# Gated mix of segment attention and a gated MLP: the order of the first loads, of four key transposes and of some dummy matmuls is changed

## The chip, the cores and the metric

One core of a Trainium2 chip runs the whole kernel. The metric is device time in microseconds (us) of one execution; before the change the median of three runs is 287.96 us (287.41 to 287.99).

## The reference, cut to what matters

The input `x` has 2048 tokens of 512 features in bf16. Two branches read it and are mixed by one gate per token.

```
g = sigmoid(sum(x * gate_w))                       # one number per token
out = g * A(x) + (1 - g) * B(x)
A: q, k, v = x@wq, x@wk, x@wv; 32 heads of 16; 4 segments of 512 tokens
   for each segment s:
     a_dot = softmax(q k^T / 4 + causal mask) v    # inside the segment
     a_mem = phi(q) M / (phi(q) z + 1e-6)          # memory of the earlier segments
     o = sigmoid(beta) * a_mem + (1 - sigmoid(beta)) * a_dot
     M += phi(k)^T v;  z += sum(phi(k))            # phi(t) = t+1 if t>0 else exp(t)
   A = o @ wo
B: h = relu(x@W_gate) * (x@W_up)   (1792 wide);  B = h @ W_down
```

## The kernel before

Everything stays in SBUF. `xT` holds x transposed (features on partitions) in four chunks of 512 tokens, one per segment. The work of segment s is: the projections `proj(s)` (L550), attention `att(s)` (L643: 20 "quads" of scores, an exponential of 128x2048 on ScalarE for each, a causal mask on GpSimd, then P V), the update of the memory `mu(s)` (L593), the read of the memory `nd(s)` (L611), the gated MLP `ffn(s)` (L716) and the output product `outp(s)` (L740).

No engine's program is written by hand. Each operation is an `Op` with a cost and the names it reads and writes; `Sched` (L85) is a list scheduler that runs while the kernel is built. It keeps a clock for each engine, takes the ready operation of the best queue (a lower number is preferred), and so fixes the order of the instructions on every engine and the semaphore waits. An operation may not be placed before the planner's clock says that what it reads is there; for a transfer that is L264 to L266: bytes at 330 GB/s after the transfers before it, plus 1800 ns. On the chip each engine then runs its fixed list in order, each instruction waiting for its semaphores.

What the change touches:

- Loads. `load` (L412) puts a transfer on SP's or ScalarE's list. x chunk 0 comes first (four blocks of 128 tokens), then `wq`, `wk`, `wv`, each as two transfers by halves of the contracted dimension ("a": rows 0 to 255 on SP, "b": rows 256 to 511 on ScalarE). On SP follow `beta`, the first halves of W_gate and W_up, the gate weights, four transposing loads of x chunk 1 (`load_x`, L431 to L434), the second halves of W_gate and W_up, `wo`, `wd`, and eight transposing loads of x chunks 2 and 3. All of that is one queue of priority 0 (L454, L455).
- Chunk 0 of `xT` is made on TensorE: after five dummy matmuls into `psA0` (`warm`, L480) come four groups of four transposing matmuls into the banks of `psL` (L491), and one copy of 128x512 per group, on VectorE (L496) or ScalarE (L497). Every projection matmul of segment 0 waits for all four copies.
- `proj(s)` issues, for each of four column groups G, a q group and a k group of four matmuls (L563), cut in two pairs over the contracted dimension; the first pair reads half "a" of the weight, the second half "b". For v it is the same with tokens on the partitions (L561).
- phi(k) of a group is written into `ek[G]` by VectorE (L583) and then transposed by a DMA on SP into `phik[G]` (L584). `mu(s)` has two halves; the first (`mu0_0`, L602) reads `phik[0]`, `phik[1]` and v, and the last half of the MLP, all scores and so on stand behind it on TensorE as the planner has ordered them. The next segment's exponential of k overwrites `ek` (L581).
- The gate for chunks 1 to 3 is one operation of 48 small matmuls (`gmm1`, L519), which reads x chunks 1, 2 and 3.

Of the kernel before, what the change touches and what calls it, by code (L numbers as in the profile page):

```python
# [7 lines left out]
ACT = mybir.ActivationFunctionType  # L8
# [5 lines left out]
LAT = 60.0  # L14
PE_LAT = 175.0
SWITCH = 100.0
WARM = 5


def mm(n, k=1):  # L20
# [3 lines left out]
def t_act(n, psum=True, ap=0):  # L24
    return (174.0 if psum else 198.0) + 0.834 * n + 93.0 * ap


def t_dve(n, rate=1):
    return 155.0 + n / rate / 0.96
# [25 lines left out]

class Op:
    __slots__ = ("engs", "eng", "fns", "occs", "lat", "reads", "writes", "name", "dma", "nbytes", "mode", "ep", "role",
                 "preds", "stream", "idx", "start", "end", "done", "cidx")

    def __init__(self, alts, reads=(), writes=(), name="", lat=0.0, dma=False, nbytes=0, mode="f", ep=None, role=None):  # L60
        self.engs = [a[0] for a in alts]
        self.fns = {a[0]: a[1] for a in alts}
        self.occs = {a[0]: float(a[2]) for a in alts}
        self.eng = self.engs[0] if len(alts) == 1 else None
        self.lat = lat
        self.reads = tuple(reads)
        self.writes = tuple(writes)
        self.name = name
        self.dma = dma
        self.nbytes = nbytes  # L70
        self.mode = mode
        self.ep = ep
        self.role = role
        self.preds = []
        self.stream = self.idx = self.start = self.end = None
        self.done = False
        if ep is not None:
            if role == "r":
                ep.readers.append(self)
                self.reads = self.reads + (ep.res,)  # L80
            else:
                self.writes = self.writes + (ep.res,)


class Sched:  # L85
# [113 lines left out]

    def ready(self, op, e):  # L200
        t0 = self.now[e]
        t = 0.0
        for p in self._pred_done(op, e):
            if not p.done:
                return None
            if self.know[e][p.stream] < p.idx:
                t = max(t, p.end + LAT)
        if op.ep is not None:
            if op.role == "w" and op.ep.bank is None:
                for rd in op.ep.readers:  # L210
                    for p, _ in rd.preds:
                        if p.ep is op.ep or p.cidx > op.cidx:
                            continue
                        if not p.done:
                            return None
                        t = max(t, p.end - op.occs["pe"] - 300.0)
                bc = self._bank_choice(op, e)
                if bc is None:
                    return None
                t = max(t, bc[1])  # L220
            elif op.ep.bank is None:
                return None
        if e == "pe" and t > 0:
            t += 80.0
        return max(t, t0)
# [12 lines left out]
    def place(self, op, e, start):  # L238
        op.eng = e
        if op.ep is not None and op.role == "w" and op.ep.bank is None:  # L240
            bi, _ = self._bank_choice(op, e)
            prev = self.bank_ep[bi]
            if prev is not None:
                for r in prev.readers:
                    op.preds.append((r, False))
            self.bank_ep[bi] = op.ep
            op.ep.bank = bi
        deps = {}
        for p in self._pred_done(op, e):
            deps[p.stream] = max(deps.get(p.stream, 0), p.idx)  # L250
        self._waits(e, deps)
        occ = op.occs[e]
        if e == "pe":
            if op.mode != self.mode or start > self.now[e] + 60.0:
                occ += SWITCH
            self.mode = op.mode
        if op.dma:
            d = min(range(self.ndma), key=lambda i: (self.dma_end.get(i, 0.0), i))
            st = f"dma{d}"
            if self.cnt[st] > 0:  # L260
                self._waits(e, {st: self.cnt[st]})
            self.cnt[st] += 1
            inc = 16
            issued = start + occ  # L264
            self.dma_busy = max(self.dma_busy, issued) + op.nbytes / 330.0
            op.end = self.dma_busy + 1800.0  # L266
            self.dma_end[d] = op.end
        else:
            st = e
            self.cnt[st] += 1  # L270
            inc = 1
            op.end = start + occ + op.lat
        idx = self.cnt[st]
        self.prog[e].append(("ins", op, st, inc))
        op.stream, op.idx, op.start, op.done = st, idx, start, True
        sn = dict(self.know[e])
        sn[st] = max(sn[st], idx)
        self.snap[st][idx] = sn
        self.now[e] = start + occ
        self.busy[e] += occ  # L280
        self.log.append((start, start + occ, e, op.name))
# [98 lines left out]
def program(sc, nc, T, PL, PA, A_x, A_wq, A_wk, A_wv, A_wo, A_beta, W_g, W_u, W_d, gate_w, out, NSEG, KT, NF, NT, EPS, SCALE):  # L380
# [5 lines left out]
    def pe(fn, occ, **k):  # L386
        k.setdefault("lat", PE_LAT)
        if k.get("role") == "w":
            k["reads"] = list(k.get("reads", ())) + [f"init{i}" for i in range(4)]
        return op("pe", fn, occ, **k)  # L390
# [14 lines left out]
        return PA[ep.bank]  # L405

    def xt(c):
        return [f"xT{c}_{kt}" for kt in range(KT)]

    lact, lsp = [], []  # L410

    def load(eng, names, dst, src, nbytes, occ=460.0):  # L412
        (lact if eng == "act" else lsp).append(dma(eng, lambda e, dst=dst, src=src: e.dma_start(dst, src), nbytes, occ=occ, writes=names, name="ld" + names[0]))  # L413
    x0 = A_x[0, 0:512, :].rearrange("(i p) d -> p i d", p=128)
    for i, eng in enumerate(("sp", "act", "sp", "act")):
        load(eng, [f"hT{i}"], V.hT[:, i, :], x0[:, i, :], 1 << 17)
    for nm, w, src in (("wq", V.wq, A_wq), ("wk", V.wk, A_wk), ("wv", V.wv, A_wv)):
        r = src.rearrange("(kt p) n -> p kt n", p=128)
        load("sp", [nm + "a"], w[:, 0:2, :], r[:, 0:2, :], 1 << 18)
        load("act", [nm + "b"], w[:, 2:4, :], r[:, 2:4, :], 1 << 18)  # L420
    wgr = W_g.rearrange("(kt p) n -> p kt n", p=128)
    wur = W_u.rearrange("(kt p) n -> p kt n", p=128)
    half = (NF // 2) * 128
# [20 lines left out]
    load_gu(1)  # L444
    load("sp", ["wo"], V.wo[:], A_wo.rearrange("(g p) n -> p g n", p=128), 1 << 19)
    load("sp", ["wd"], V.wd[:], W_d.rearrange("(f p) n -> p f n", p=128), NF * 128 * 1024)
    for c in range(2, NSEG):
        load_x(c)
    sc.queue(0, lact)
    sc.queue(0, lsp)  # L450

    st = []
    st.append(pool(lambda e: e.memset(V.ident[:], 1.0), 150, writes=["ident"], name="id0"))
# [23 lines left out]
    ds.append(dve(lambda e: e.reduce_sum(V.pm[:, :], pm8, AX.X), 180, reads=["pm8"], writes=["pm"], name="pm"))  # L477
    sc.queue(0, ds)

    def warm(n, k):  # L480
        def fn(e):
            for i in range(n):
                ins = e.matmul(PA[0][:, :], lhsT=V.rl[:, 0, 0:128], rhs=V.rl[:, 0, :], start=True, stop=True)
            return ins
        return pe(fn, n * 427, reads=["rl0"], writes=["init0"], name=f"warm{k}")

    xps, xcs = [warm(WARM, 0)], []
    for i in range(4):
        def fx(e, i=i):
            for kt in range(KT):  # L490
                ins = e.matmul(PL[:, i, kt * 128:(kt + 1) * 128], lhsT=V.hT[:, i, kt * 128:(kt + 1) * 128], rhs=V.ident[:], start=True, stop=True)  # L491
            return ins
        xps.append(pe(fx, 430, reads=[f"hT{i}", "ident"], writes=[f"bankL{i}"], name=f"xt{i}"))
        dst = V.xT[:, :, i * 128:(i + 1) * 128]
        srcp = PL[:, i, :].rearrange("q (k t) -> q k t", k=KT)
        xcs.append(sc.add(Op([("dve", lambda e, d=dst, s_=srcp: e.tensor_copy(d, s_), t_dve(512)),  # L496
                              ("act", lambda e, d=dst, s_=srcp: e.activation(d, s_, ACT.Copy), t_act(512))],  # L497
                             reads=[f"bankL{i}"], writes=[f"xT0_{i}"], name=f"xc{i}")))
    sc.queue(0, xps)
    sc.queue(0, xcs)  # L500

    cst = [act(lambda e: e.activation(V.eb[:], V.braw[:], ACT.Exp), 300, reads=["braw"], writes=["eb"], name="eb")]
    cst.append(dve(lambda e: e.tensor_scalar(V.romgh[:], V.eb[:], 1.0, None, ALU.add), 190, reads=["eb"], writes=["romgh"], name="romgh"))
# [46 lines left out]
    def proj(s):  # L550
# [3 lines left out]
        def pj(w, col, name, wname, tokmajor=False):  # L554
            ep = Epoch("proj")

            for k0 in range(0, KT, 2):
                def fn(e, k0=k0):
                    for kt in (k0, k0 + 1):
                        if tokmajor:  # L560
                            ins = e.matmul(A(ep)[:, :], lhsT=V.xT[:, kt, tok + col * 128:tok + (col + 1) * 128], rhs=w[:, kt, :], start=(kt == 0), stop=(kt == KT - 1))  # L561
                        else:
                            ins = e.matmul(A(ep)[:, :], lhsT=w[:, kt, col * 128:(col + 1) * 128], rhs=V.xT[:, kt, tok:tok + 512], start=(kt == 0), stop=(kt == KT - 1))  # L563
                    return ins
                pes.append(pe(fn, mm(512, 2), reads=[wname + ("b" if k0 else "a")] + xt(s), name=f"{name}{s}_{col}", ep=ep, role="w2" if k0 else "w"))
            return ep
        for G in range(4):
            ep = pj(V.wq, G, "q", "wq")
# [284 lines left out]
```

## Time and profile before

| | |
|---|---|
| median of 3 runs | 287.96 us (287.41 to 287.99) |
| profiled execution | 287.23 us, its span 285.8 us |
| PE busy | 267.7 us (94%) |
| DVE busy | 197.3 us (69%) |
| ACT busy | 194.5 us (68%) |
| POOL busy | 92.1 us (32%) |
| chain that ended last | PE 78%, SPq 13%, issue 3%, ACT 3%, DVE 2%, DMA 1% |
| mean granted TensorE clock | 0.982 |

PE is TensorE's matmuls, PEld its weight loads, DVE VectorE, ACT ScalarE, POOL GpSimd, SPq the queue in which SP issues transfers. "Busy" is the time in which an engine has an instruction in work. The span runs from the first to the last instruction; the execution's own time is 1.43 us more. "Issue" in a chain or a wait is time for which the trace names no releaser. The granted clock is a share of TensorE's full 2.4 GHz.

### The profile page before, as it was taken

Reading aid. Unit: us, or ns where it says so; the run is one execution under the profiler, and the core shown is the slowest. Engines: PE = TensorE matmul, PEld = TensorE weight load, DVE = VectorE, ACT = ScalarE, POOL = GpSimd, SP = SyncE. Lnnn points to the kernel's source line nnn. Section 1 sums busy time; section 2 is a strip of 40 time slices with the busy share of each in tenths; the row PEclk is TensorE's granted clock in tenths of the full one; section 3 lists DMA queues with packets and bytes.
Section 4 is the critical chain, followed back from the end, with each engine's and each line's share of the span. In section 5 each row is a group of like instructions: output and inputs, shape, how many; then the busy total and the mean of one; then the engine's idle time right before and its main releaser. Section 6 shows DMA issues by size and latency. Waiting matters only on the chain.

```text
span 285.8 us, 5289 instructions
## 1 busy us (share of the span) xinstructions
PE 267.7 (94%) x2145; PEld 116.0 (41%) x2181; DVE 197.3 (69%) x383; ACT 194.5 (68%) x173; POOL 92.1 (32%) x152
## 2 busy tenths in 40 slices
PE   6999919999989999999999999999999999999995
PEld 3343314444444444444344444433434433434442
DVE  5598824999988999766878783659573619597300
ACT  3268825978795887777857996777777768784211
POOL 4002211336243445452423433333243333341000
PEclk9999966999999999999999999999999999999999
DMA  7999950010000162100001200000011100000011
GB/s 230 323 210 368 183 105 2 0 40 0 21 20 20 21 86 46 37 21 18 2 0 37 39 20 21 18 21 0 2 37 37 34 23 21 0 2 2 2 37 37
DMA packets 29240, 15.29 MB, mean 54 GB/s; under 512 B 20768, under 2 KB 29216, under 8 KB 29216
## 3 DMA queue, kind: packets, MB, share of 16 engines
q1 hardware_dynamic: 28112, 13.91, 20.4%
q10 hardware_dynamic: 1104, 1.05, 1.1%
q8 instruction: 17, 0.28, 0.4%
q14 instruction: 7, 0.06, 0.1%
HBM read 8.14 MB, written 2.10 MB: 36 GB/s over the span
## 4 chain that ended last, share of the span: by engine, by line
PE 78%; SPq 13%; issue 3%; ACT 3%; DVE 2%; DMA 1%; ACTq 0%; DVEq 0%
PE psA L726 30%; PE psA L757 16%; SPq L433 10%; PE psL L656 8%; PE psA L681 7%; PE psA L563 5%; PE psA L749 5%; PE psA L561 4%; SPq L413 2%; ACT E L661 2%; PE psA L602 1%; PE psA L631 1%; DMA phik<-ek 1%; DVE hT L737 1%; PE psA L519 0%
## 5 line engine op out<-in xcount | busy, mean ns | idle before, releaser
L661 ACT ACTIVATE E<-psL 128x2048 bf16<-128x2048 f32 x80 | 150.1, 1876 | 37.0 <-PE psL L656 36.6
L664 POOL TENSOR_SCALAR_AFFINE_SELECT E<-E 128x512 bf16<-128x512 bf16 x128 | 82.3, 661 | 159.3 <-ACT E L661 159.3
L726 PE MATMUL psA<-xT,wg 128*128 128x512 bf16 x215 | 59.0, 384 | 1.2 <-issue 1.1
L726 PE MATMUL psA<-xT,wu 128*128 128x512 bf16 x215 | 58.6, 384 | 1.1 <-DVE omg L526 0.3
L757 PE MATMUL psA<-wd,hT 128*128 128x512 bf16 x216 | 52.8, 380 | 1.1 <-issue 1.0
L737 DVE TENSOR_TENSOR hT<-psA,rl 128x512 bf16<-128x512 f32 x56 | 38.4, 686 | 15.1 <-PE psA L726 11.6
L686 DVE STREAM_TRANSPOSE Tn<-psA 128x512 f32<-128x512 f32 x32 | 21.4, 697 | 19.6 <-PE psA L681 19.5
L656 PE MATMUL psL<-qT,kp 32*128 32x384 bf16 (+3 forms) x512 | 31.9, 302 | 1.0 <-ACT E L661 0.8
L726 PEld LDWEIGHTS psA<-xT,wu 128*128 128x128 bf16 x224 | 20.8, 99 | 26.3 <-issue 3.6
L734 ACT ACTIVATE rl<-psA 128x512 bf16<-128x512 f32 x33 | 19.6, 595 | 15.8 <-PE psA L726 14.9
L726 PEld LDWEIGHTS psA<-xT,wg 128*128 128x128 bf16 x224 | 20.0, 99 | 25.4 <-issue 5.4
L757 PEld LDWEIGHTS psA<-wd,hT 128*128 128x128 bf16 x224 | 20.2, 98 | 24.7 <-issue 3.7
L656 PEld LDWEIGHTS psL<-qT,kp 32*128 32x128 bf16 x512 | 8.9, 92 | 33.1 <-ACT E L661 21.6
L681 PE MATMUL psA<-E,vaug 128*17 128x256 bf16 (+3 forms) x512 | 21.0, 300 | 0.0
L563 PE MATMUL psA<-xT,wq 128*128 128x512 bf16 x60 | 16.9, 401 | 1.4 <-DVE xT L496 0.9
L735 DVE TENSOR_SCALAR rl<-psA 128x512 bf16<-128x512 f32 x23 | 15.8, 686 | 2.9 <-PE psA L726 2.3
L563 PE MATMUL psA<-xT,wk 128*128 128x512 bf16 x61 | 17.2, 396 | 0.4 <-DVE ttmp L582 0.2
L762 ACT ACTIVATE osb<-psA,omg 128x512 bf16<-128x512 f32 x10 | 6.9, 687 | 15.3 <-PE psA L757 15.3
L749 PE MATMUL psA<-wo,oT 128*128 128x512 bf16 x62 | 16.0, 379 | 0.2 <-issue 0.2
L561 PE MATMUL psA<-wv,xT 128*128 128x512 bf16 x63 | 15.3, 380 | 0.2 <-issue 0.2
L681 PEld LDWEIGHTS psA<-E,vaug 128*17 128x17 bf16 x512 | 10.5, 90 | 10.8 <-issue 4.2
L581 ACT ACTIVATE ek<-kT 128x512 bf16<-128x512 bf16 x12 | 7.5, 627 | 9.6 <-DMA phik<-ek 5.5
(68 smaller groups left out, 213.9 us busy)
## 6 DMA issues: line engine op xcount, KB each, us to landing
out_dram<-osb SPq DMA_DIRECT2D x16, 128.0 KB, 1.7
wg<-in_B_W_gate_dram SPq DMA_DIRECT2D x2, 896.0 KB, 7.3
wu<-in_B_W_up_dram SPq DMA_DIRECT2D x2, 896.0 KB, 9.6
wd<-in_B_W_down_dram SPq DMA_DIRECT2D x1, 1792.0 KB, 14.2
wo<-in_A_wo_dram SPq DMA_DIRECT2D x1, 512.0 KB, 9.6
hT<-in_A_x_dram ACTq DMA_DIRECT2D x2, 128.0 KB, 3.1
hT<-in_A_x_dram SPq DMA_DIRECT2D x2, 128.0 KB, 2.8
wq<-in_A_wq_dram SPq DMA_DIRECT2D x1, 256.0 KB, 4.4
```

The costliest lines, as they stand in the source:

```text
L433: lsp.append(dma("sp", lambda e, c=c, kt=kt: e.dma_start_transpose(V.xT[:, kt, c * 512:(c + 1) * 512], A_x[0, c * 512:(c + 1) * 512, kt * ...
L561: ins = e.matmul(A(ep)[:, :], lhsT=V.xT[:, kt, tok + col * 128:tok + (col + 1) * 128], rhs=w[:, kt, :], start=(kt == 0), stop=(kt == KT - 1))
L563: ins = e.matmul(A(ep)[:, :], lhsT=w[:, kt, col * 128:(col + 1) * 128], rhs=V.xT[:, kt, tok:tok + 512], start=(kt == 0), stop=(kt == KT - 1))
L656: ins = q.matmul(PL[:, jj, o:o + w], lhsT=V.kp[32 * jj:32 * jj + 32, kslot(s, n), 128 * j:128 * j + 128], rhs=V.qT[32 * jj:32 * jj + 32, q ...
L661: acts.append(act(lambda a, e=e: a.activation(V.E[:, e, :, :], PL[:, :, :], ACT.Exp, scale=SCALE), t_act(2048), reads=[f"bankL{b}" for b i ...
L664: pools.append(pool(lambda g, ap=ap: g.affine_select(out=ap, in_=ap, compare_op=ALU.is_ge, fill=0.0, base=0, pattern=[[0, 4], [1, 128]], c ...
L681: ins = q.matmul(A(ep)[32 * jj:32 * jj + 17, c:512], lhsT=V.vaug[:, s % 2, j, 8 * G + 2 * jj + p, :], rhs=V.E[:, e, jj, o:o + w], start=(j ...
L686: ds.append(dve(lambda e, p=p, ep=eps[p]: e.transpose(V.Tn[:, p, :], A(ep)[:, :]), t_dve(512), writes=[f"Tn{p}"], name=f"tr{s}_{G}_{p}", e ...
L726: ins = e.matmul(A(ep)[:, :], lhsT=w[:, kt, f * 128:(f + 1) * 128], rhs=V.xT[:, kt, c * 512:(c + 1) * 512], start=(kt == 0), stop=(kt == K ...
L737: evs.append(dve(lambda e, ep=eu, r=r, hs=hs: e.tensor_tensor(V.hT[:, hs, :], A(ep)[:, :], V.rl[:, r, :], ALU.mult), t_dve(512), reads=[f" ...
L749: ins = e.matmul(A(ep)[:, :], lhsT=V.oT[:, o0 + G, i * 128:(i + 1) * 128], rhs=V.wo[:, G, :], start=(G == 0), stop=False)
L757: ins = e.matmul(A(ep)[:, :], lhsT=V.hT[:, slots[f], i * 128:(i + 1) * 128], rhs=V.wd[:, f, :], start=False, stop=(f == NF - 1))
```

## The change

The planner gets an earliest time per operation (`after`), and other costs for transfers. Loads of `wq` and `wk` are cut by output columns (columns 0 to 255 and 256 to 511; `wq` on SP, `wk` on ScalarE); the `wv` halves stay. The loads of x chunks 2 and 3 leave the first SP list; they form a queue of priority 3 with earliest planner times of 30000 and 40000 ns, while the `phik` transposes keep priority 1. The dummy matmuls go to a bank of `psL` (so they no longer wait for the clearing of `psA0`), one more stands behind the transposing matmuls, and each copy to `xT` is cut into two halves, the first on VectorE, the second on ScalarE. The projections wait for the column half that they read.

```diff
     def ready(self, op, e):
         t0 = self.now[e]
-        t = 0.0
+        t = op.after
...
-            self.dma_busy = max(self.dma_busy, issued) + op.nbytes / 330.0
-            op.end = self.dma_busy + 1800.0
+            self.dma_busy = max(self.dma_busy, issued) + op.nbytes / 310.0
+            op.end = self.dma_busy + (1800.0 if start < 4000.0 else 3200.0)
...
-    for nm, w, src in (("wq", V.wq, A_wq), ("wk", V.wk, A_wk), ("wv", V.wv, A_wv)):
-        r = src.rearrange("(kt p) n -> p kt n", p=128)
-        load("sp", [nm + "a"], w[:, 0:2, :], r[:, 0:2, :], 1 << 18)
-        load("act", [nm + "b"], w[:, 2:4, :], r[:, 2:4, :], 1 << 18)
+    for h in range(2):
+        for nm, w, src, eng in (("wq", V.wq, A_wq, "sp"), ("wk", V.wk, A_wk, "act")):
+            load(eng, [f"{nm}{h}"], w[:, :, 256 * h:256 * h + 256], src.rearrange("(kt p) n -> p kt n", p=128)[:, :, 256 * h:256 * h + 256], 1 << 18)
+    for h, eng in enumerate(("sp", "act")):
+        load(eng, [f"wv{h}"], V.wv[:, 2 * h:2 * h + 2, :], A_wv.rearrange("(kt p) n -> p kt n", p=128)[:, 2 * h:2 * h + 2, :], 1 << 18)
...
+    sc.queue(0, lact)
+    sc.queue(0, lsp)
+    lsp = []
     for c in range(2, NSEG):
         load_x(c)
-    sc.queue(0, lact)
-    sc.queue(0, lsp)
+        for t in lsp[-KT:]:
+            t.after = 30000.0 + 10000.0 * (c - 2)
+    sc.queue(3, lsp)
...
-    def warm(n, k):
+    def warm(n, k, b):
         def fn(e):
             for i in range(n):
-                ins = e.matmul(PA[0][:, :], lhsT=V.rl[:, 0, 0:128], rhs=V.rl[:, 0, :], start=True, stop=True)
+                ins = e.matmul(PL[:, b, :], lhsT=V.rl[:, 0, 0:128], rhs=V.rl[:, 0, :], start=True, stop=True)
             return ins
-        return pe(fn, n * 427, reads=["rl0"], writes=["init0"], name=f"warm{k}")
+        return pe(fn, n * 427, reads=["rl0"], writes=[f"bankL{b}"], name=f"warm{k}")
-    xps, xcs = [warm(WARM, 0)], []
+    xps, xcs = [warm(5, 0, 3)], []
...
-        xcs.append(sc.add(Op([("dve", lambda e, d=dst, s_=srcp: e.tensor_copy(d, s_), t_dve(512)),
-                              ("act", lambda e, d=dst, s_=srcp: e.activation(d, s_, ACT.Copy), t_act(512))],
+        for h in range(2):
+            dst = V.xT[:, 2 * h:2 * h + 2, i * 128:(i + 1) * 128]
...
+            if h == 0:
+                xcs.append(dve(lambda e, d=dst, s_=srcp: e.tensor_copy(d, s_), t_dve(256), reads=[f"bankL{i}"], writes=[f"xT0_{i}a"], name=f"xc{i}"))
+            else:
+                xcs.append(act(lambda e, d=dst, s_=srcp: e.activation(d, s_, ACT.Copy), t_act(256), reads=[f"bankL{i}"], writes=[f"xT0_{i}b"], name=f"xc{i}"))
+    xps.append(warm(1, 1, 0))
...
-                pes.append(pe(fn, mm(512, 2), reads=[wname + ("b" if k0 else "a")] + xt(s), name=f"{name}{s}_{col}", ep=ep, role="w2" if k0 else "w"))
+                pes.append(pe(fn, mm(512, 2), reads=[f"{wname}{k0 // 2 if tokmajor else col // 2}"] + xt(s), name=f"{name}{s}_{col}", ep=ep, role="w2" if k0 else "w"))
```

## Rows read from the trace of the kernel before

**Rows 1.** Windows by stage: length, busy us (instructions) of each engine, clock, DMA share, GB/s.
```profile
0.00:6.74 6.74, 4.02 (x21) 2.41 (x22) 3.65 (x8) 2.48 (x3) 3.40 (x15) 1.00 0.73 222
6.74:10.69 3.95, 3.95 (x10) 1.35 (x11) 1.03 (x2) 0.01 (x1) 0.00 (x0) 1.00 0.83 285
...
35.56:41.81 6.25, 0.02 (x1) 0.00 (x0) 1.81 (x4) 0.78 (x3) 1.22 (x2) 0.69 0.49 103
41.81:48.24 6.43, 6.06 (x68) 3.71 (x70) 2.80 (x11) 3.17 (x4) 1.39 (x2) 0.50 0.11 23
...
80.00:285.80 205.80, 197.94 (x1619) 84.80 (x1644) 136.50 (x247) 142.53 (x107) 70.01 (x109) 1.00 0.10 22
```

**Rows 2.** Chain of waits around 19 to 42 us: start, us, what.
```profile
19.10 9.05 SPq L433
...
28.19 1.46 SPq L433
...
37.98 2.50 DMA phik<-ek
40.49 1.36 issue
```

**Rows 3.** Timeline of TensorE, 41 to 49 us, half clock: start, us, engine, line, [idle before].
```profile
41.85 1.07 PE L602 MATMUL psA<-vaug,phik 128*128 128x136 bf16 x8 [6.26 <-issue]
...
44.10 0.61 PE L656 MATMUL psL<-qT,kp 32*128 32x512 bf16 x4
...
45.47 0.15 PEld L726 LDWEIGHTS psA<-xT,wu 128*128 128x128 bf16 x1 [0.28 <-issue]
...
48.03 0.15 PEld L726 LDWEIGHTS psA<-xT,wu 128*128 128x128 bf16 x1 [0.28 <-issue]
```

**Rows 4.** Timeline of VectorE and GpSimd, 27 to 36 us.
```profile
27.10 1.40 POOL L664 TENSOR_SCALAR_AFFINE_SELECT E<-E 128x512 bf16<-128x512 bf16 x2 [1.95 <-ACT E L661]
27.15 0.86 DVE L583 TENSOR_TENSOR ek<-ek,ttmp 128x512 bf16<-128x512 bf16 x1
...
29.17 0.41 DVE L583 TENSOR_TENSOR ek<-ek,ttmp 128x512 bf16<-128x512 bf16 x1
...
35.36 0.41 DVE L583 TENSOR_TENSOR ek<-ek,ttmp 128x512 bf16<-128x512 bf16 x1
```

**Rows 5.** DMA view, transposing loads issued at 29.70 and at 36.68: us to landing.
```profile
xT<-in_A_x_dram SPq DMA_TRANSPOSE x1, 5.2
...
xT<-in_A_x_dram SPq DMA_TRANSPOSE x1, 3.0
```

**Rows 6.** Timeline of TensorE at full clock, 20 to 80 us.
```profile
21.16 1.03 PE L726 MATMUL psA<-xT,wu 128*128 128x512 bf16 x4
...
79.43 0.64 PE L602 MATMUL psA<-vaug,phik 128*128 128x136 bf16 x8
```

**Rows 7.** Timeline of the first 10 us: start, us, engine, line, [idle before].
```profile
1.84 2.31 PE L483 MATMUL psA<-rl 128*128 128x512 bf16 x5 [1.84 <-DVE psA L476]
...
3.95 1.91 PE L491 MATMUL psL<-ident,hT 128*128 128x128 bf16 x16
...
5.90 0.69 DVE L496 CAST xT<-psL 128x512 bf16<-128x512 f32 x1 [0.16 <-PE psL L491]
...
6.74 1.86 PE L563 MATMUL psA<-xT,wq 128*128 128x512 bf16 x4 [0.88 <-DVE xT L496]
```

**Rows 8.** DMA view, `wq`, both halves issued at 1.73 us.
```profile
wq<-in_A_wq_dram SPq DMA_DIRECT2D x1, 256.0 KB, 4.4
wq<-in_A_wq_dram ACTq DMA_DIRECT2D x1, 256.0 KB, 5.7
```

**Rows 9.** Windows in three stretches between 20 and 80 us, columns as in rows 1.
```profile
20.00:35.56 15.56, 15.24 (x93) 6.01 (x92) 13.54 (x31) 13.60 (x17) 3.90 (x6) 1.00 1.18 284
35.56:50.00 14.44, 7.84 (x100) 4.42 (x104) 5.34 (x17) 5.45 (x10) 2.61 (x4) 0.65 0.26 55
50.00:80.00 30.00, 29.42 (x264) 12.64 (x263) 28.93 (x61) 25.41 (x22) 12.19 (x19) 1.00 0.09 19
```

More of the change, by code (lines that the diff above doesn't have):

```diff
@@ L16 @@
 SWITCH = 100.0
-WARM = 5
 def mm(n, k=1):
@@ L57 @@
     __slots__ = ("engs", "eng", "fns", "occs", "lat", "reads", "writes", "name", "dma", "nbytes", "mode", "ep", "role",
-                 "preds", "stream", "idx", "start", "end", "done", "cidx")
+                 "after", "preds", "stream", "idx", "start", "end", "done", "cidx")
     def __init__(self, alts, reads=(), writes=(), name="", lat=0.0, dma=False, nbytes=0, mode="f", ep=None, role=None):
@@ L73, in __init__ @@
         self.role = role
+        self.after = 0.0
         self.preds = []
@@ L407, in xt @@
     def xt(c):
-        return [f"xT{c}_{kt}" for kt in range(KT)]
+        return [f"xT{c}_{kt}" for kt in range(KT)] if c else [f"xT0_{i}{h}" for i in range(4) for h in "ab"]
     lact, lsp = [], []
@@ L493, in program @@
         xps.append(pe(fx, 430, reads=[f"hT{i}", "ident"], writes=[f"bankL{i}"], name=f"xt{i}"))
-        dst = V.xT[:, :, i * 128:(i + 1) * 128]
-        srcp = PL[:, i, :].rearrange("q (k t) -> q k t", k=KT)
-        xcs.append(sc.add(Op([("dve", lambda e, d=dst, s_=srcp: e.tensor_copy(d, s_), t_dve(512)),
-                              ("act", lambda e, d=dst, s_=srcp: e.activation(d, s_, ACT.Copy), t_act(512))],
-                             reads=[f"bankL{i}"], writes=[f"xT0_{i}"], name=f"xc{i}")))
+        for h in range(2):
+            dst = V.xT[:, 2 * h:2 * h + 2, i * 128:(i + 1) * 128]
+            srcp = PL[:, i, 256 * h:256 * h + 256].rearrange("q (k t) -> q k t", k=2)
+            if h == 0:
[3 more added lines that the diff above has]
+    xps.append(warm(1, 1, 0))
     sc.queue(0, xps)
-    sc.queue(0, xcs)
+    sc.queue(0, [t for t in xcs if t.eng == "dve"])
+    sc.queue(0, [t for t in xcs if t.eng == "act"])
     cst = [act(lambda e: e.activation(V.eb[:], V.braw[:], ACT.Exp), 300, reads=["braw"], writes=["eb"], name="eb")]
```

## The prediction

> **What bounds the kernel now.** Read the windows by stage first. From 80 us to the end TensorE is busy 197.9 of 205.8 us at full clock [rows 1], so there the time is the sum of TensorE's work and a change of loads can do nothing. Two earlier stages differ. From 35.56 to 41.81 us TensorE does nothing for 6.25 us, VectorE works 1.81 us and ScalarE 0.78; and in the 6.43 us behind it TensorE is busy again, but at a granted clock of 0.50, that is 1.2 instead of 2.4 GHz [rows 1]. A third piece is the start. For 6.74 to 10.69 the clock column says 1.00, but ten matmuls in 3.95 us [rows 1] are 0.395 each, nearly the pace of the half clock below; the rise is taken where the pace doubles, about 10.69.
>
> What ended the idle time is in the chain of waits. It runs through SP: a transposing load of x chunk 2 stands in issue from 19.10 for 9.05 us, seven more follow from 28.19 (9.8 us, 1.4 each), only at 37.98 does the first `phik` transpose begin, and 40.49 plus 1.36 is where the second has landed and TensorE starts [rows 2]. The instruction that waited is the first half of the memory update, with 6.26 us of idle time before it [rows 3]. What these transposes read was ready long before: VectorE's L583 for groups 0 and 1 ended at 27.15 + 0.86 = 28.01 and 29.17 + 0.41 = 29.58 [rows 4]. So TensorE waited for a queue, not for work, and x chunks 2 and 3, for which it waited, were needed only by `gmm1` behind it.
>
> **The change part by part.** The profiled execution took 287.23 us, of which 285.8 are the span; the sum is made on that.
>
> (a) The eight x transposes leave the place ahead of `phik`. After `wd` SP's list has `phik` 0, which waits for 28.01, and `phik` 1, which waits for 29.58. Priority and the earliest times of 30000 and 40000 ns put x 2 and 3 behind these; `phik` 2, ready at 35.36 + 0.41 = 35.77 [rows 4], may come between them and is read only by the second half of the update. The queue still holds `wd` then, so the landing is not the bare 2.5 us of [rows 2]. The nearest row is the x transpose issued at 29.70, which landed 5.2 us later, at 34.9; one issued at 36.68, with the weights gone, took 3.0 [rows 5]. So `phik` 1 lands between 29.6 + 2.5 = 32.1 and 34.9, before TensorE comes to it at 35.56. The idle time goes whole: -6.25. Its upper bound stands among the rivals.
>
> (b) With no gap the clock has no reason to fall. The clock fell only while TensorE stood idle [rows 1]. In the 6.43 us at half clock, the weight loads of consecutive 512-column matmuls stand at 45.47, 48.03 and five places between, six steps in 2.56 us, 0.427 each [rows 3]; at twice the clock that is 0.214, and four such matmuls at full clock, with the last one's tail, took 1.03 [rows 6]. From the quad's end at 44.10 + 0.61 = 44.7 to 48.24 there are 3.5 / 0.427 = 8.3 of them, each 0.213 dearer: 1.77. The eight matmuls of the memory update took 1.07 against 0.64 later [rows 3, 6]: 0.43. The quad's four, 0.61 [rows 3], I put at a third less, 0.2. The 48 one-column matmuls of `gmm1` I put at nothing, since their cost sits in the weight loads. Sum -2.4; bounds 0 and half of 6.43, 3.2.
>
> (c) The start. The dummies no longer wait for VectorE's clearing of `psA0`, which released them at 1.84; the transposing matmuls run 3.95 to 5.86 and the last copy is 5.90 to 6.59, the projection begins at 6.74 [rows 7]. Halving the copy onto two engines saves about half of its 0.69, 0.35, and the transposes may begin earlier too. The new order needs `wq`'s first column half at once, where the old needed half "b" only for its third matmul, and half "b" landed at 1.73 + 5.7 = 7.43 [rows 8]. Half "a" on SP, which has the new half's place, landed at 1.73 + 4.4 = 6.1 [rows 8]. If the new half comes as late as 7.43, the projection begins at 7.5, 0.8 late; if it comes at 6.1, at 6.2, 0.55 early. At half clock each of these is worth half: +0.4 to -0.3. I take -0.1. The column halves move the same bytes in rows of half the length; no row prices that by itself, and the late bound, 1.3 us after half "a", covers it. Behind the waiting projection the whole of TensorE's list stands, so its delay is the delay of all. The sixth dummy lies in time in which TensorE would wait.
>
> (d) What is late next. With the gap out, VectorE loses its rest. From 35.56 to 50 it works 5.34 us; that stretch shrinks to 14.44 - 8.65 = 5.8 us. From 20 to 80 it has 13.54 + 5.34 + 28.93 = 47.81 us of work [rows 9] for 60.0 - 8.65 = 51.35, 93%; from 50 to 80 it ran at 96% while TensorE kept 98% [rows 9], so it can bear that, but without slack. Bounds: nothing; and 2.5 us, a little over its backlog when TensorE stopped (it had 1.81 us left to do [rows 1]). I take +0.6, near the lower end, because the row with 96% shows TensorE hardly held up.
>
> `gmm1`, x 2 and x 3 move behind: the planner's own clock releases x 3 at 40000 ns, four issues of 1280 and a landing of 3200 later `gmm1` may stand at 48.3 us of that clock, and what hangs on it (the gate of segments 1 to 3) is used in segment 1. I put that at nothing; its cover is attention and the MLP of segment 0, and the price without it is the last rival. The other planner costs reorder operations of independent work; no row prices that, so it is left inside the range.
>
> Sum: -6.25 - 2.4 - 0.1 + 0.6 = -8.15 on 287.23, 279.1. The median of the three runs is 0.73 above the profiled execution; halfway between the two bases, 279.4.
>
> **Rules weighed.** On the start the rows show half clock although TensorE had been at work, with gaps, from 1.84: ten projection matmuls at 0.395 up to 10.69 [rows 1, 7], and the full pace in [rows 6]. The Trainium skill, in TensorE: Matmul & The Clock Gate, under "What's actually happening", says that activity releases the throttle and that the watch runs freely, so that the same kernel can rise at another point in another run. By that rule the rise is no fixed 10.69, and (c) would be anything up to rival 1; the trace, one execution, can't show it.
>
> Beside VectorE's L583 at 27.15, which took 0.86, stand two GpSimd masks from 27.10 for 1.40; the one at 29.17 took 0.41 [rows 4]. The Trainium skill, in SBUF — State Buffer, under "Who interferes with whom", says that a VectorE instruction with two SBUF inputs and a GpSimd one that reads SBUF exclude each other for a whole instruction. By it a closer packing brings more such pairs and speaks against the change; the trace agrees with 0.45 lost on that one. The whole of it would lie inside (d)'s bounds.
>
> **Rivals.**
> 1. The clock rises earlier, since the dummies begin sooner and another one fills the wait. For it: the gap of 0.88 before 6.74 [rows 7] is the only long one there. Against: the wait for `wq` may stay. In 6.74 to 10.69 ten matmuls ran [rows 1]; at full clock they save ten times 0.213, 2.1, less what the weights' landing takes back, so about 1.8: 277.6.
> 2. Chunk 2 slips in between `phik` 0 and `phik` 1. For it: `ek` 1 was ready at 29.58 [rows 4], close to the 30000 ns at which x 2 is let go, though that is the planner's clock. Then four transposes of 1.4 us [rows 2] go first, 29.4 to 35.0, `phik` 1 lands at 35.0 + 2.5 = 37.5, and TensorE idles 2 us, plus up to 2.4 if the clock falls again: 281.4 to 283.8; 282.4.
> 3. VectorE becomes the bound between 35 and 75 us and the full 2.5 us of (d) is paid, 1.9 more than the forecast: 281.3. Against: its 93%.
> 4. The release does nothing, because `phik` is held up behind something else as long as now: 287.96. Only SP's queue speaks for it, and the rows show `ek` ready and SP the last to come.
> 5. Slower: `gmm1` keeps its place right behind the first memory update, and TensorE waits there for x 3. Then from 28.0 SP issues `phik` 0 and 1, x 2 and 3, ten at 1.4 us [rows 2]; the last x begins to be issued at 40.6 and, with `phik` 2 in between, at 42.0, and lands 3.0 later [rows 5], at 45. TensorE, there at 36.1, idles 8.9, then runs at half clock as now: -6.25 - 2.4 + 8.9 + 2.4 + 0.5 = +3.2 on 287.23, 290.4. It decides when TensorE reaches `gmm1` before x 3 lands; against it the 48.3 us on the planner's clock.
>
> **How the numbers follow.** Forecast 0.55, early clock 0.14, VectorE 0.11, chunk 2 first 0.10, `gmm1` 0.06, nothing 0.04. The time is the forecast's, 279.4. The forecast with its own bounds, (b) 0 to 0.8 better, (c) 0.3 either way, (d) 0.6 better to 1.9 worse, spans 278 to 282; rival 1 takes the low end to 276.8, rivals 2 and 3 the high end to 283.3, and outside are rivals 4 and 5 and tails, some 0.15. A change of 0.2%, 0.6 us, is about what three runs that spread 0.58 can tell. Faster: 0.55 + 0.14 + 0.11 + 0.10 = 0.90; same 0.04; slower 0.06.
>
> **What would show it.** Right: SP's list has two `phik` transposes straight behind `wd`, no idle time over 1 us on TensorE between 20 and 60 us, granted clock 1.00 from its rise on, `gmm1` after 45 us. Wrong in (a): idle time before L602 or L519. Wrong in (b): a second stretch at 0.50. Wrong in (c): the first projection after 7 us. Wrong in (d): TensorE waiting for VectorE, with VectorE over 97% between 30 and 70. Waits for x chunk 2 in segment 2's projections would also break the forecast.

## The result, and the profile after

The changed kernel takes 278.95 us (median of four, 277.56 to 279.81) against 287.98; the ratio is 0.9679, 95% interval [0.9632, 0.9727]. A second set of six runs gave 278.09 and 0.9659 [0.9616, 0.9701]. The forecast was 279.4. The profiled execution took 279.81, its span is 278.1, 7.7 us less than before. It was the slowest of its four, and the profiled one before, 287.23, was faster than the timed runs beside it, so the two traces differ by less (7.4 us) than the medians do (9.0 and 9.7).

Windows by stage of the changed kernel, columns as in [rows 1], the lines answering to [rows 1, 9]:

```profile
0.00:5.65 5.65, 4.36 (x22) 2.31 (x22) 3.66 (x10) 2.14 (x4) 3.42 (x15) 1.00 0.57 165
5.65:9.06 3.41, 1.13 (x6) 0.48 (x6) 0.31 (x1) 0.68 (x2) 0.00 (x0) 1.00 0.96 285
9.06:12.48 3.42, 3.42 (x10) 1.24 (x9) 1.74 (x3) 0.61 (x2) 0.00 (x0) 0.50 0.91 331
12.48:30.00 17.52, 17.52 (x121) 7.11 (x120) 15.31 (x40) 15.37 (x23) 5.11 (x8) 1.00 1.08 294
30.00:40.00 10.00, 10.00 (x95) 4.00 (x93) 9.93 (x21) 8.56 (x9) 4.22 (x6) 1.00 0.47 117
40.00:60.00 20.00, 20.00 (x192) 9.22 (x193) 17.85 (x41) 17.18 (x18) 7.72 (x12) 1.00 0.19 41
60.00:80.00 20.00, 20.00 (x187) 8.35 (x185) 18.40 (x41) 15.24 (x16) 9.40 (x13) 1.00 0.07 15
```

From 12.48 to 80 us TensorE has no idle time and full clock: the gap of 6.25 us and the half clock behind it are gone, although VectorE is busy 99% of 30 to 40. The stage at half clock is now at the start. The record of the granted clock begins at 5.65 with full clock (the 1.00 ahead of it stands where there is no record), but from there to 9.06 TensorE worked only 1.13 us, and then it had half clock until 12.48.

Timeline of TensorE in the changed kernel: the first projection, and the two instructions that followed the gap before (L611 is the update, L528 `gmm1`; old L602 and L519):

```profile
8.13 1.02 PE L572 MATMUL psA<-xT,wq 128*128 128x512 bf16 x4 [2.28 <-DMA wq<-in_A_wq_dram]
...
8.99 1.84 PE L572 MATMUL psA<-xT,wk 128*128 128x512 bf16 x4
...
47.17 0.65 PE L611 MATMUL psA<-vaug,phik 128*128 128x136 bf16 x8
...
53.27 1.34 PE L528 MATMUL psA<-gwc,xT 128*128 128x1 bf16 x48
```

The first projection begins at 8.13, 1.39 later than in [rows 7], after waiting 2.28 us for `wq`. Its column half was issued at 1.73 and landed 6.3 us later (timeline of SP's queue and DMA view of loads issued from 1.6 to 2.0, the changed kernel):

```profile
1.73 0.98 SPq L413 DMA_DIRECT2D wq<-in_A_wq_dram  x2
...
wq<-in_A_wq_dram SPq DMA_DIRECT2D x1, 256.0 KB, 6.3
```

Neither the update nor `gmm1` waits, but both stand later: 47.17 against 41.85 in [rows 3].

Timeline of SP's queue in the changed kernel, answering to [rows 2] (L593 are the `phik` transposes, L434 those of x):

```profile
19.43 0.83 SPq L413 DMA_DIRECT2D wd<-in_B_W_down_dram  x1
31.36 1.22 SPq L593 DMA_TRANSPOSE phik<-ek  x1
32.62 6.10 SPq L434 DMA_TRANSPOSE xT<-in_A_x_dram  x4
41.03 1.22 SPq L593 DMA_TRANSPOSE phik<-ek  x1
```

This is not the order that was forecast. x chunk 2 goes between `phik` 0 and `phik` 1, and `phik` 1 is issued at 41.03, later than the 37.98 at which `phik` 0 began before. It could not be issued sooner: VectorE now finishes `ek` 1 only at 41.00 (timeline of VectorE, the changed kernel, answering to [rows 4]):

```profile
40.59 0.41 DVE L592 TENSOR_TENSOR ek<-ek,ttmp 128x512 bf16<-128x512 bf16 x1
```

Does the account close? In full-clock time, between the first projection and 12.48 us TensorE did 3.95 / 2 + 1.79 = 3.76 us of work before, and 0.93 + 3.42 / 2 = 2.64 after: 1.1 lost. Against the 6.25 us of the gap and the forecast's 2.4 for the half clock that leaves 7.5 of the 7.7 found between these two executions; with the 1.9 that keepclock measures below it leaves 7.0, and 0.7 stays open. Of the medians' 9.0 and 9.7 us, 0.9 and 1.6 stay open beyond 6.25 + 1.9.

### The profile page after: what moved, and what is told of

Same layout as the page of the kernel before. It is cut to its first block, busy times and chain, and to the rows that moved or that the text cites. A ratio compares the mean times of both kernels' runs of the same rounds, so it can differ in the third digit from the quotient of the medians.

```text
span 278.1 us, 5326 instructions
## 1 busy us (share of the span) xinstructions
PE 270.1 (97%) x2182; PEld 115.1 (41%) x2182; DVE 197.3 (71%) x389; ACT 192.0 (69%) x171; POOL 94.5 (34%) x152
## 4 chain that ended last, share of the span: by engine, by line
PE 94%; DMA 2%; ACT 2%; SPq 0%; DVE 0%; issue 0%; DVEq 0%; ACTq 0%
PE psA L735 36%; PE psA L766 18%; PE psA L572 11%; PE psL L665 10%; PE psA L690 7%; PE psA L570 5%; PE psA L758 5%; DMA wq<-in_A_wq_dram 2%; ACT E L670 1%; PE psA L611 1%; PE psA L640 1%; PE psA L528 1%; SPq L413 0%; DVE hT L746 0%; ACT osb L771 0%
## 5 line engine op out<-in xcount | busy, mean ns | idle before, releaser
L673 POOL TENSOR_SCALAR_AFFINE_SELECT E<-E 128x512 bf16<-128x512 bf16 x128 | 84.0, 675 | 147.2 <-ACT E L670 145.6
L735 PE MATMUL psA<-xT,wg 128*128 128x512 bf16 x224 | 60.1, 380 | 0.0
L735 PE MATMUL psA<-xT,wu 128*128 128x512 bf16 x224 | 59.4, 380 | 0.0
L766 PE MATMUL psA<-wd,hT 128*128 128x512 bf16 x224 | 55.6, 380 | 0.9 <-DVE hT L746 0.9
L572 PE MATMUL psA<-xT,wq 128*128 128x512 bf16 x64 | 17.7, 396 | 2.3 <-DMA wq<-in_A_wq_dram 2.3
L770 DVE TENSOR_SCALAR osb<-psA,omg 128x512 bf16<-128x512 f32 x8 | 5.9, 736 | 16.0 <-PE psA L766 16.0
L579 DVE CAST qT<-psA 128x512 bf16<-128x512 f32 x16 | 11.0, 690 | 5.8 <-PE psA L572 5.5
```

Of the source, the lines that this page charges most:

```text
L673: pools.append(pool(lambda g, ap=ap: g.affine_select(out=ap, in_=ap, compare_op=ALU.is_ge, fill=0.0, base=0, pattern=[[0, 4], [1, 128]], c ...
L735: ins = e.matmul(A(ep)[:, :], lhsT=w[:, kt, f * 128:(f + 1) * 128], rhs=V.xT[:, kt, c * 512:(c + 1) * 512], start=(kt == 0), stop=(kt == K ...
L766: ins = e.matmul(A(ep)[:, :], lhsT=V.hT[:, slots[f], i * 128:(i + 1) * 128], rhs=V.wd[:, f, :], start=False, stop=(f == NF - 1))
```

## The experiments

Three questions were open. Did the time come from SP's order, as predicted, or from the later place of the update on TensorE? Was the half clock worth 2.4? And what is the new start worth? Each of three sets was run beside the kernel before, whose medians there are 287.98, 287.79 and 287.56.

**SP's order alone (move).** The kernel before with this edit, and nothing else of the change:

```diff
-        t = 0.0
+        t = op.after
...
+    sc.queue(0, lact)
+    sc.queue(0, lsp)
+    lsp = []
     for c in range(2, NSEG):
         load_x(c)
-    sc.queue(0, lact)
-    sc.queue(0, lsp)
+        for t in lsp[-KT:]:
+            t.after = 30000.0 + 10000.0 * (c - 2)
+    sc.queue(3, lsp)
```

> Before, with the x move alone (x chunks 2 and 3 in the queue of priority 3 with their earliest times; transfer costs, weight loads, dummies and copies as before). SP's list now has phik 0 and 1 straight behind wd, and TensorE's list has the first memory update even a little earlier than before. Theory SP (the prediction's step a: the update waited only for x ahead of phik on SP): phik 1 lands at 32 to 35 us, TensorE idles at L602's counterpart 0 to 1.7 us, no half clock after the start, 287.98 - 8.65 + 1 = about 280 (278.5 to 281.5). Theory ORDER (the time was gained because the planner put the first update and gmm1 later on TensorE, not because phik comes earlier): with the update at its old place the wait stays, at least 4 us of it, 285 or more.

Measured: 280.28 us, ratio 0.9736 [0.9695, 0.9778]. SP's queue, then TensorE (timelines of this kernel; L589 is `phik`, L607 the update):

```profile
19.00 0.96 SPq L414 DMA_DIRECT2D wd<-in_B_W_down_dram  x1
28.38 2.77 SPq L589 DMA_TRANSPOSE phik<-ek  x2
31.19 5.18 SPq L434 DMA_TRANSPOSE xT<-in_A_x_dram  x4
```

```profile
33.69 0.40 PE L661 MATMUL psL<-qT,kp 32*128 32x384 bf16 x8
34.02 0.65 PE L607 MATMUL psA<-vaug,phik 128*128 128x136 bf16 x8
34.50 1.03 PE L568 MATMUL psA<-xT,wk 128*128 128x512 bf16 x4
```

Here the forecast's step (a) happens to the letter: two `phik` transposes straight behind `wd`, and the update, even earlier than before, waits for nothing. Theory ORDER falls as the only explanation: the later place is not needed.

**The planner's transfer costs alone (costs)**, which move the update later but leave x ahead of `phik`:

```diff
-            self.dma_busy = max(self.dma_busy, issued) + op.nbytes / 330.0
-            op.end = self.dma_busy + 1800.0
+            self.dma_busy = max(self.dma_busy, issued) + op.nbytes / 310.0
+            op.end = self.dma_busy + (1800.0 if start < 4000.0 else 3200.0)
```

> Before, with the planner's transfer costs alone (310 GB/s and 3200 ns); x chunks 2 and 3 stay ahead of phik on SP. In this kernel's list TensorE's first memory update stands some 10 us later than before and gmm1 about 1.5 us later than the old update. Theory ORDER: no wait at the update although phik 0 still begins only at about 38 us; what is left is a wait of 2 to 4 us at gmm1 for x chunk 3, which lands at about 41, perhaps with half clock behind it: 281 to 284.5. Theory SP: the update waits as before, 287 to 288.5.

Measured: 284.36 us, 0.9878 [0.9841, 0.9914]. Timeline of TensorE in this kernel:

```profile
37.15 1.03 PE L726 MATMUL psA<-xT,wu 128*128 128x512 bf16 x4
41.04 1.34 PE L519 MATMUL psA<-gwc,xT 128*128 128x1 bf16 x48 [2.86 <-issue]
...
51.09 0.65 PE L602 MATMUL psA<-vaug,phik 128*128 128x136 bf16 x8
```

The update no longer waits, but `gmm1` does, 2.86 us. The trace names no releaser; SP's queue speaks for x chunk 3, whose last transpose left that queue just before the first `phik`, at 38.93. So the order on TensorE can also take the wait away, but only in part while x 2 and 3 stay where they were.

**Both, without the new start (movecosts, mc_again):** the two diffs above together.

> Before, with the x move and the transfer costs together, but weight loads by row halves, dummies and copies as before: the change without its start. Theory LATE HALF (in the changed kernel wq's column half lands at 8.0 us instead of 6.1 and 7.4, the projection starts 1.4 us later, which costs about 1.1): first projection at 6.7 us again, 278.95 - 1.1 = about 277.8. Rival (the new start is worth what was predicted, 0.1 to 0.3 faster): 279.1 to 279.3. No idle time at the memory update or gmm1 in either.

Measured: 279.10 us, 0.9695 [0.9657, 0.9734]; the second time (below) 279.49. That is what the whole change gives, within the noise. It is 1.2 below move, with overlapping intervals, so it isn't shown that the costs add anything to SP's order. The late half was not the 1.1 us that theory LATE HALF put on it, and the first projection began at 7.12, not 6.7.

**The earliest times taken out of the changed kernel (noafter).**

```diff
-            t.after = 30000.0 + 10000.0 * (c - 2)
+            t.after = 0.0
```

> The changed kernel without the earliest times of 30000 and 40000 ns; the loads of x chunks 2 and 3 keep their own queue of priority 3. On SP's list they stand straight behind wd again, since nothing else is ready there on the planner's clock. Theory (the earliest times do the work, the priority none): phik 0 begins at about 38 us, gmm1 waits 2.5 to 3.5 us for x chunk 3, as with the transfer costs alone, 283.5 to 284.5. Rival (the priority is enough): 278 to 279.

Measured: 282.62 us, 0.983 [0.9779, 0.9882]. SP's queue of this kernel:

```profile
19.64 0.51 SPq L413 DMA_DIRECT2D wd<-in_B_W_down_dram  x1
20.19 17.73 SPq L434 DMA_TRANSPOSE xT<-in_A_x_dram  x8
37.96 3.88 SPq L593 DMA_TRANSPOSE phik<-ek  x3
```

All eight x transposes are ahead of `phik` again and `gmm1` waits, in this profile 1.81 us, with half clock after it:

```profile
39.79 1.39 PE L528 MATMUL psA<-gwc,xT 128*128 128x1 bf16 x48 [1.81 <-issue]
```

The time is 0.9 below the range expected, in line with a wait 1.0 us shorter than in costs. The priority of 3 alone leaves SP's order as it was: this planner fills an idle queue with whatever is ready, and only an earliest time keeps it free.

**The half clock by itself (keepclock).** The kernel before, with dummies ahead of the gap; the lists of all engines are otherwise the same:

```diff
+                        if name == "q" and s == 1 and col == 3 and kt == 0:
+                            for _ in range(24):
+                                e.matmul(A(ep)[:, :], lhsT=w[:, 0, 0:128], rhs=V.xT[:, 0, tok:tok + 512], start=True, stop=True)
```

> Before, with 24 dummy matmuls of 512 columns put in front of the last q projection ahead of the gap (into its own bank, which the projection then overwrites); they fill 5.2 of the 6.25 idle us, the wait for phik stays. Theory (step b: half clock behind the gap costs 2.4 us): no second stretch at 0.50, first update at about 41.8 us still, 287.8 - 2.4 = 285.4 (285 to 286.2, since the last q projection comes 5 us later). Rival (the half clock cost little, the gap was all): 287.3 to 288.2.

Measured: 285.70 us, 0.9934 [0.9903, 0.9964], 1.9 us less than the 287.56 beside it. Windows of this kernel, the gap and what follows, and the update in its timeline of TensorE:

```profile
33.00:41.00 8.00, 7.27 (x41) 3.15 (x35) 2.64 (x6) 2.75 (x4) 1.22 (x2) 1.00 0.58 121
41.00:48.24 7.24, 6.92 (x115) 4.12 (x116) 5.72 (x17) 6.10 (x9) 1.55 (x3) 1.00 0.09 19
...
40.90 0.63 PE L605 MATMUL psA<-vaug,phik 128*128 128x136 bf16 x8 [0.68 <-issue]
```

In this execution the clock stays at 1.00 through the wait; the update begins at 40.90, 0.95 earlier than in [rows 3], as SP's first `phik` was issued at 37.05 here in place of 37.98. It was the fastest of the twelve and one of two at a mean clock of 1.000. The other ten had 0.992 to 0.994 (the sixteen beside them 0.974 to 0.988), so some half clock remained in them, and no trace shows where. Useless work inside a wait that remains made the kernel faster; (b) is confirmed in kind, at 1.9 us with an interval of 1.0 to 2.8, and the 2.4 forecast lies within it.

**The start, part by part (cols; after_again, rows, mccols, mc_again).** Column halves alone on the kernel before:

```diff
+    for h in range(2):
+        for nm, w, src, eng in (("wq", V.wq, A_wq, "sp"), ("wk", V.wk, A_wk, "act")):
+            load(eng, [f"{nm}{h}"], w[:, :, 256 * h:256 * h + 256], src.rearrange("(kt p) n -> p kt n", p=128)[:, :, 256 * h:256 * h + 256], 1 << 18)
...
-                pes.append(pe(fn, mm(512, 2), reads=[wname + ("b" if k0 else "a")] + xt(s), name=f"{name}{s}_{col}", ep=ep, role="w2" if k0 else "w"))
+                pes.append(pe(fn, mm(512, 2), reads=[f"{wname}{k0 // 2 if tokmajor else col // 2}"] + xt(s), name=f"{name}{s}_{col}", ep=ep, role="w2" if k0 else "w"))
```

> Before, with the weight loads by column halves alone. Theory LATE HALF: wq's first half lands at 8.0 us or later, the first projection starts at 8 us and the start costs 0.9 to 1.2 us. This kernel's list also puts the first memory update later (behind gmm1, which stands where the update stood), so TensorE waits for x chunk 3 until about 41 us at gmm1 in place of the update: some 6 us of idle time and half clock behind it, about 288 to 289.5. Rival (the halves land as the old ones did, and what was late in the changed kernel was something else, as the dummies or the copies): first projection at 6.2 to 6.8 us, 287 to 288.

Measured: 287.29 us, 0.9978 [0.9946, 1.0011]. Timeline of TensorE in this kernel:

```profile
7.29 1.86 PE L564 MATMUL psA<-xT,wq 128*128 128x512 bf16 x4 [1.42 <-DMA wq<-in_A_wq_dram]
...
40.42 1.42 PE L520 MATMUL psA<-gwc,xT 128*128 128x1 bf16 x48 [4.98 <-issue]
```

As expected `gmm1` waits in place of the update, so the column halves as such changed the planner's order. The first projection, at 7.29, fits neither theory's range, the time only the rival's. Then four kernels in one set, made of the same edits: with the weight loads by column or row halves (in `rows` the diff above is undone), and with or without the new dummies and copies.

> The changed kernel once more, beside the three that follow. Theory NIL (the new start is worth nothing either way, and the late first projection of 8.13 us in its profile was one draw of a landing that varies): 278.5 to 279.3, first projection between 6.5 and 8.2 us. Theory LATE (the column halves land later every time and cost about 1 us, which the dummies and the split copies give back in part): 278.9 as well, but first projection at 7.8 us or later again.

> The changed kernel with the weight loads by row halves as before. Theory NIL: 278.5 to 279.3, no difference from the changed kernel over 0.4 us. Theory LATE: first projection at 6.2 to 6.8 us, 1 us faster than the changed kernel, 277.9.

> The changed kernel without its dummies and split copies (x move, transfer costs, column halves). Theory NIL: 278.7 to 279.5. Theory LATE: the column halves cost their 1 us and nothing gives it back: 279.6 to 280.2, first projection at 7.8 us or later. If the dummies are worth something by the clock, the granted clock rises earlier in the changed kernel than here.

> x move and transfer costs alone, measured at 279.1 in the earlier set, beside the other three. Theory NIL: 278.7 to 279.5, like all. Theory LATE: 278.6 to 279.1, with 'rows' faster by what dummies and copies are worth.

| | column halves | row halves |
|---|---|---|
| new dummies and copies | 278.09 (after_again), 0.9659 [0.9616, 0.9701] | 278.75 (rows), 0.9679 [0.9637, 0.9721] |
| old | 277.86 (mccols), 0.9650 [0.9601, 0.9699] | 279.49 (mc_again), 0.9702 [0.9659, 0.9745] |

All intervals overlap, and each kernel spreads over 2.1 to 2.5 us. Theory LATE fails: `rows` is no faster, and the column kernels are 0.7 and 1.6 lower in the median, which these runs can hint at but not prove; they lie 0.4 and 0.8 below theory NIL's ranges, the row kernels inside them. The first projection began at 7.58 (after_again), 7.07 (rows), 6.50 (mccols) and 6.98 (mc_again). The landing of `wq` varies from execution to execution; the 6.3 us in the changed kernel's first profile was the longest of the six profiles with column halves (4.7 to 6.3).

**The wait for `wq` filled (fill8).** What does make the spread? Of ten runs of the changed kernel four had a mean granted clock of 0.993 or 0.994 and took 278.93 to 279.81 (mean 279.28), six had 0.999 or more and took 277.12 to 278.77 (mean 277.86). In both profiled runs of the first kind the half clock lies behind the wait for `wq`. The changed kernel with eight dummies instead of the single one:

```diff
-    def warm(n, k, b):
+    def warm(n, k, b, real=0):
         def fn(e):
-            for i in range(n):
+            for i in range(real or n):
...
-    xps.append(warm(1, 1, 0))
+    xps.append(warm(1, 1, 0, 8))
```

> The changed kernel with eight dummy matmuls in place of the single one behind the transposing matmuls (the lists of all engines stay as they are). Theory CLOCK (the spread of the changed kernel is the clock: the runs at a mean clock of 0.993 or 0.994, whose first full-clock stretch is lost again while TensorE waits for wq, are 1.4 us slower than those at 0.999): no run below 0.998, median 277.6 to 278.0, longest run under 278.8. Rival (the clock's draw has nothing to do with that wait): some runs at 0.994 still, median 278.1 to 278.9. If the dummies overrun the landing of wq, the first projection begins after 8.2 us and up to 0.5 is lost.

Measured: 277.76 us, six runs from 277.68 to 278.17, all at 0.998 or more; 0.9650 [0.9611, 0.9690]. Timeline of TensorE in this kernel:

```profile
5.19 2.06 PE L488 MATMUL psL<-rl 128*128 128x512 bf16 x8
7.53 1.02 PE L572 MATMUL psA<-xT,wq 128*128 128x512 bf16 x4 [0.29 <-DMA wq<-in_A_wq_dram]
8.39 1.03 PE L572 MATMUL psA<-xT,wk 128*128 128x512 bf16 x4
```

The wait shrinks to 0.29 us, the first projections run at full pace (1.02 for four), and the spread falls from 2.1 (after_again) to 0.5 us. The mean clock isn't the whole of the spread, though: the six runs of mccols, without any of the new dummies, were all at 0.998 or more and still spread 2.5 us, and a late first rise doesn't enter the mean, as the record begins with it (the profiled run of `rows` has a mean of 1.000, though its first projections ran at half clock). This is the lowest median of all versions, by 0.1 us; against the changed kernel's two medians, 278.95 and 278.09 in other sets, its gain in the median isn't shown, that in the spread is.

## Why the prediction was right, and where it was not

- **(a), the gap goes whole: right in size, and its way is one of two.** The 6.25 us are gone. In the changed kernel it isn't by the order that was named: of "`phik` 0, which waits for 28.01, and `phik` 1, which waits for 29.58" straight behind `wd` only the first came so. The step that failed is the 29.58: it is a time of the old list. The planner's new costs, which the prediction left inside the range, gave VectorE another list, with `ek` 1 done at 41.00 (movecosts has the changed kernel's order on SP too, move hasn't). The order is rival 2's, without its price, since the same costs put the update at 47.17, behind the late `phik` 1. With SP's order alone the named way occurs (move). What both ways share, and what the costs alone lack, is that `gmm1` is not held up by x 2 and 3.
- **`gmm1` and rival 5: rightly put at nothing.** It stands at 53.27 and waits for nothing; the planner's earliest time kept it back, as said. The costs alone, the column halves alone and noafter show the rival's mechanism, at 2.86, 4.98 and 1.81 us.
- **(b): right in kind; put at 2.4, measured at 1.9** by keepclock, with an interval of 1.0 to 2.8 and some half clock left in ten of its twelve runs.
- **(c), the start: wrong in the profiled execution.** It was put at -0.1 with +0.4 as the late end; there it cost 1.1. The step that failed is the bound "as late as 7.43": it came at 1.73 + 6.3 = 8.0. One landing had been read as a property of the load, and it varies from run to run. By the prediction's own halving the delay of 1.39 costs 0.7; the other 0.4 is half clock until 12.48 in place of 10.69, for which (c) had no term. In the medians no worth of the new start can be told, so -0.1 is neither confirmed nor refuted.
- **(d), VectorE: 0.6 forecast, nothing found.** At 99% in 30 to 40 us TensorE didn't wait for it.
- **Rival 1, the early clock, is a mechanism that occurs,** but the dummies don't decide it: mccols, without the new ones, ran its first four projections in 1.02 us at 6.50, `rows`, with them, in 1.86 at 7.07. In the profiled run of the changed kernel it came at 5.65 and was lost after the wait. Nor does the kernel decide it: movecosts and mc_again are one kernel, and the first ran its first four projections at half clock, the second its first two at full clock. The prediction's rule from the Trainium skill (TensorE: Matmul & The Clock Gate, "What's actually happening") that the same kernel can rise at another point in another run agrees with this. Timelines of TensorE, in the order rows, mccols, movecosts, mc_again:

```profile
7.07 1.86 PE L571 MATMUL psA<-xT,wq 128*128 128x512 bf16 x4 [1.37 <-DMA wq<-in_A_wq_dram]
...
6.50 1.02 PE L569 MATMUL psA<-xT,wq 128*128 128x512 bf16 x4 [1.00 <-DMA wq<-in_A_wq_dram]
...
7.12 1.87 PE L568 MATMUL psA<-xT,wq 128*128 128x512 bf16 x4 [1.26 <-DMA wq<-in_A_wq_dram]
...
6.98 0.59 PE L568 MATMUL psA<-xT,wq 128*128 128x512 bf16 x2 [1.11 <-DMA wq<-in_A_wq_dram]
```

- Of the signs named in advance, no idle time over 1 us between 20 and 60 and `gmm1` after 45 came true; two `phik` transposes straight behind `wd`, and full clock from the rise on, did not. The sign against (c), a first projection after 7 us, came at 8.13. That the time came out 0.5 from the forecast is in part luck: in the traces (c), and by its middle value (b), were too hopeful and (d) too careful, and the medians fell by 0.9 and 1.6 us more than the sum of -8.15, which no term explains.

## What to carry to other kernels

Find the wait first, then ask which transfer ahead of the awaited one nobody needs yet; moving that one was worth here the wait, 6.25 us, plus the clock that the wait cost, about 1.9. In a planned kernel a lower priority does not hold a transfer back from an idle queue, an earliest time does. Where a wait can't be removed, dummy matmuls inside it can still pay (1.9 us here); in the first microseconds they bought steadiness, and no shown gain in the median.

## What the runs showed of the hardware

Idle stretches of 2.28 us (the changed kernel, before 8.13), 2.86 (costs) and 1.81 (noafter) were each followed by a stretch of half clock. At the start the length of the wait alone doesn't decide it. In costs, waits of 1.02 us before 6.53 and 0.42 before 7.54 were followed by half clock, in mc_again waits of 1.11 before 6.98 and 0.39 before 7.96 were not (timelines of TensorE, costs and then mc_again):

```profile
8.32 1.93 PE L563 MATMUL psA<-xT,wk 128*128 128x512 bf16 x4 [0.17 <-DMA wk<-in_A_wk_dram]
...
8.41 0.60 PE L568 MATMUL psA<-xT,wk 128*128 128x512 bf16 x2
```

The landing of the first 256 KB of `wq` on SP's queue ranged from 4.4 to 5.4 us by row halves and from 4.7 to 6.3 by column halves over the profiles, with the same transfers ahead of it.
